# Seven passes for VectorE's exponentials, and six score banks a unit on VectorE in the final layer, in a four-layer attention kernel

## The chip, the core and the metric

The kernel runs on one core of a Trainium2 chip. The core has five engines with their own instruction queues: TensorE (PE, with its weight loads shown as PEld), VectorE (DVE), ScalarE (ACT), GpSimd (POOL) and SyncE (SP), and 16 DMA engines that they issue transfers to. TensorE writes its results into PSUM, eight banks of 128 partitions x 2 KB; a bank holds one 128x512 tile of fp32. The metric is device time in microseconds (us) of one launch, the median of several.

## The reference

The input is a sequence of 2048 rows of width 640, in bf16. Four layers run one after the other, A, B, A, B, each `x = x + attention(layernorm(x))`, with 32 heads of 20 elements. Layers A (numbers 0 and 2 in the kernel) let a query see only the 256 keys up to its own; layers B (1 and 3) let every query see all 2048 keys:

```python
scores = jnp.einsum("bhqd,bhkd->bhqk", q, k) * (Dh ** -0.5)
p = _softmax(scores, axis=-1)
o = jnp.einsum("bhqk,bhkd->bhqd", p, v)
return (lambda x, *d: x.transpose(*d))(o, 0, 2, 1, 3).reshape(B, S, D) @ wo
```

Each layer B takes 32 x 2048 x 2048 exponentials. They are the bulk of the elementwise work.

## The kernel before

**Units, banks and tiles.** Queries are cut into four chunks `c` of 512, heads into eight groups `g` of four. A *unit* is a layer, a chunk and a group, (l, c, g). In a layer B a unit has 16 key blocks x 4 heads = 64 *banks*: one bank is the scores of 128 keys against 512 queries of one head, transposed so that keys lie on partitions. A *tile* is usually three banks: TensorE writes the scores of three banks into PSUM (L1316; banks 0 to 2 on even tiles, 3 to 5 on odd ones), ScalarE takes the exponential of all three in one instruction and writes bf16 to SBUF (L1347), and two or three tiles later TensorE multiplies them by the values (L1380) and accumulates in bank 7. On odd tiles a fourth bank, number 6, can be added if nothing else wants it (`next_tile`); such a tile is an instruction of 2048 columns that writes `ka`.

**Bank 6** has three users in the final layer: those wide tiles, the short tasks that finish units (`t_tail`: row sums, reciprocals, scaling) and chunks (`t_out`, `t_before_last`: the output projection), which take it through `take_m` and give it back with `drop_m`, and the path described next.

**The side path.** Some banks of a unit, `u.aside`, never go to ScalarE. `t_side` is a generator that computes their exponentials on VectorE, two banks (a *pair*) at a time. For each of the two it has TensorE write the scores into bank 6 (L912, in layer 3) and reads them with L918, which scales to a fixed-point number, clamps and stores int32. Then six passes over the pair's 128x1024 elements follow, all SBUF to SBUF: L923 and L928 split mantissa and exponent with bit operations, L933, L937, L941 and L949 are two-input operations that evaluate a quartic; the last multiplies by the power of two and writes bf16. That is eight instructions to a pair. In layer 3 its scratch lies in idle `xnT` buffers, its results in five slots for pairs, three in `ka` and two in `qa`; in layer 1 it uses `raw_o`. The values of the aside banks are multiplied in at the end of the unit (L1389), and a unit's slots come free then.

**The order of the work.** The whole program is emitted by one Python loop, tile by tile (`state["tick"]`), and every engine runs its queue in that order. The side path is paced by a credit: after each tile it gains `SIDE_RATE` = 1.1 (0.95 in the last chunk of layer 3, 0.4 before the final stage), is capped at 1.2, and each pass costs what its `yield` says, 0.7 or 1.2. A score needs an odd tile, credit above zero and bank 6 free (`side_now`); after a score bank 6 counts as taken for two ticks. `side_need` and `side_done` push the side path on without credit if a unit ends before its aside banks are scored or finished. The side path may work on a unit as soon as that unit's keys are loaded, ahead of ScalarE, as long as it has slots.

Besides, TensorE gets filler matmuls (L298 with `masks,ident`, from `keep_clock`) so that each tile has a fixed amount of TensorE work. The units of layer 3 run last: (3,0,g) in two parts, then (3,1,0) to (3,3,7), 24 units, with nothing else beside them but their own finishing tasks.

**Which banks are aside.** In layer 1, chunks 1 to 3, two of a unit's 64. In layer 3, chunks 1 to 3, four of them in every unit but (3,1,0), which has none; and six in the units of chunks 1 and 2 with odd g, (3,2,7) excepted. That is 23 units x 4 + 7 x 2 = 106 banks, the count of L918 on `xnT` in the profile.

Of the kernel before, what the change touches and what calls it, by code (L numbers as in the profile page):

```python
# [9 lines left out]
BF16 = mybir.dt.bfloat16  # L10
F32 = mybir.dt.float32
I32 = mybir.dt.int32
ALU = mybir.AluOpType
ACT = mybir.ActivationFunctionType

# [5 lines left out]
NT = S // P  # L21
KD = D // P
G = 8
C = 512
NC = S // C
EPS = 1e-5
SCALE = DH ** -0.5
# [2 lines left out]

E23 = 2.0 ** 23
LOG2E = 1.4426950408889634
EA, EB, EC, ED = -0.10468731, 1.17604568, 0.83196789, 0.24582313
KA = 18
SIDE_RATE = 1.1
QA = 4

PARTS = {  # L40
# [6 lines left out]
def kernel(  # L47
# [58 lines left out]
    op = ps[:, 7, :]  # L106
# [565 lines left out]
    class Unit:  # L672
        def __init__(self, l, c, g, part=None):
            self.l, self.c, self.g, self.part = l, c, g, part
            self.windowed = l % 2 == 0
            self.aside = ()
            if self.windowed:
                sets = [(m, b0, subs, j) for m, b0, subs in window_banks(c) for j in range(4)]
            else:

                if c > 0 and (l, c, g) != (3, 1, 0):
                    self.aside = tuple((NT - 1, j) for j in ((2, 3) if l == 1 else range(4)))
                    if l == 3 and (c < 3 and g % 2 and (c, g) != (2, 7)):
                        self.aside += ((NT - 2, 0), (NT - 2, 1))
                    if l == 1 and False:
                        self.aside += ((NT - 1, 0), (NT - 1, 1))
                k0, k1 = key_blocks(l, part)
                sets = [
                    (None, 0, [(kc, 0, 4, 0)], j) for kc in range(k0, k1) for j in range(4)
                    if (kc, j) not in self.aside  # L690
                ]
            n = len(sets)
            self.banks = [
                (self, j, m, b0, subs, i < 4, i >= n - 4 + len(self.aside), i == n - 1)
                for i, (m, b0, subs, j) in enumerate(sets)
            ]
# [200 lines left out]
    def t_side():  # L897

        V = nc.vector
        while aside:  # L900
            u = aside[0]
            for pair in range(len(u.aside) // 2):
                while id(u) not in loaded or (u.l == 3 and not side["late"]):
                    yield None
                for i in range(2):
                    yield "bank"
                    xi, xm, xw = side["tiles"]
                    if u.l == 3:
                        mseq[0] += 1
                        mfree[6] = (state["tick"] + 2, mseq[0])  # L910
                        kc, j = u.aside[2 * pair + i]
                        nc.tensor.matmul(  # L912
                            ps[:, 6, :], lhsT=u.k(kc, j), rhs=u.q(j, 0, 4), start=True, stop=True
                        )
                        side["psum"] = ps[:, 6, :]
                    scored = side.setdefault("scored", {})
                    scored[id(u)] = scored.get(id(u), 0) + 1
                    V.tensor_scalar(  # L918
                        out=xi.bitcast(I32)[:, i * C : (i + 1) * C], in0=side["psum"],
                        scalar1=SCALE * LOG2E * E23, scalar2=-128.0 * E23, op0=ALU.mult, op1=ALU.max,  # L920
                    )
                    yield 0.7
                V.tensor_scalar(  # L923
                    out=xm.bitcast(I32), in0=xi.bitcast(I32), scalar1=0x7FFFFF, scalar2=0x3E800000,
                    op0=ALU.bitwise_and, op1=ALU.bitwise_or,
                )
                yield 0.7
                V.tensor_scalar(  # L928
                    out=xi.bitcast(I32), in0=xi.bitcast(I32), scalar1=0x7F800000,
                    scalar2=0x40000000, op0=ALU.bitwise_and, op1=ALU.bitwise_xor,  # L930
                )
                yield 0.7
                V.scalar_tensor_tensor(  # L933
                    out=xw, in0=xm, scalar=EA, in1=xm, op0=ALU.add, op1=ALU.mult
                )
                yield 1.2
                V.scalar_tensor_tensor(  # L937
                    out=xm, in0=xw, scalar=EB, in1=xm, op0=ALU.mult, op1=ALU.add
                )
                yield 1.2  # L940
                V.scalar_tensor_tensor(  # L941
                    out=xw, in0=xw, scalar=EC, in1=xm, op0=ALU.add, op1=ALU.mult
                )
                yield 1.2
                while not side["out"]:
                    yield None
                pt = side["out"].popleft()
                po = pt.rearrange("p a b -> p (a b)")
                V.scalar_tensor_tensor(  # L949
                    out=po, in0=xw, scalar=ED, in1=xi, op0=ALU.add, op1=ALU.mult  # L950
                )
                side_out.setdefault(id(u), []).append(pt)
                yield 1.2
            aside.popleft()

    def side_step(bank):

        if side["gen"] is None:
            return False
        moved = False  # L960
        while True:
            if side.get("at") == "bank" and not bank:
                return moved
            if side["credit"] <= 0.0:
                return moved
            try:
                at = side["at"] = next(side["gen"])
            except StopIteration:
                side["gen"] = None
                return moved  # L970
            if at is None:
                return moved
            moved = True
            if at == "bank":
                if not bank:
                    return moved
                continue
            side["credit"] -= at
            if bank:
                return moved  # L980

    def side_need(u):

# [219 lines left out]
    with tc.manual_schedule():  # L1203
# [40 lines left out]
        def next_tile(t):  # L1244

            if t < len(tiles):
                return tiles[t]
            size = 3
            if side_now:
                return [banks.popleft() for _ in range(min(size, len(banks)))]  # L1250
            if t % 2 and not tails and state["held"] is None and mfree[6][0] < state["tick"]:
                if all(task.wake > state["tick"] for task in todo):
                    size = 4
            return [banks.popleft() for _ in range(min(size, len(banks)))]

# [23 lines left out]
        while ended is None or t < ended + 8:  # L1279
# [119 lines left out]
                    break  # L1399

            if n_b:
                side["credit"] = min(side["credit"] + ((SIDE_RATE if state["unit"] < index[3, NC - 1, 0, None] else 0.95) if side["late"] else 0.4), 1.2)
                side_step(False)

            if t > 0 and masked is not None:
# [71 lines left out]
```

## Time and profile before

| | us |
|---|---|
| time, median of 3 runs | 2258.31 |
| the runs | 2255.68, 2258.31, 2261.54 |
| span of the profiled execution | 2253.6 |
| ACT busy in it | 2159.6 (96%) |
| PE busy | 1946.9 (86%) |
| DVE busy | 1253.3 (56%) |
| first score of the final layer's side path (L918 on `xnT`) | starts at 1599.0 |
| last ACT instruction | 2241.8 to 2242.5 |

The profile gives the span from the first to the last instruction; the median of the timed runs is 4.7 us above the span. PE's busy time holds the filler matmuls. In group lines a row is: line, engine, operation, output <- input, shapes, count | busy us in all, mean ns of one | idle us of the engine before them and who ended it. Instructions of one engine overlap a little, so busy time divided by count is less than the mean duration of one. In window lines a row is the stretch in us from the span's start, its length, and the busy us (and instructions) of each engine, then TensorE's granted clock and the DMA's share.

### The profile page before, as it was taken

The numbers are of one execution on the slowest core, as the hardware profiler recorded it, in microseconds if no ns is written. First come the engines' busy times: TensorE is split into PE (matmuls) and PEld (weight loads), VectorE is DVE, ScalarE is ACT, GpSimd is POOL, SyncE is SP. The second block draws the span as 40 slices with busy tenths as digits, with TensorE's granted clock in tenths as the row PEclk, the third lists the DMA queues.
The fourth block names the chain that finished last, engine by engine and source line by source line (L and its number), as shares of the span: only waits on it lengthen the run. The fifth ranks groups of instructions, "written<-read, shape, count | busy, mean of one in ns | idle before, by whom it ended". The sixth has DMA issues, their size and how long they took to land.

```text
span 2253.6 us, 71223 instructions
## 1 busy us (share of the span) xinstructions
PE 1946.9 (86%) x30991; PEld 775.9 (34%) x30991; DVE 1253.3 (56%) x2150; ACT 2159.6 (96%) x1736; POOL 484.2 (21%) x950
## 2 busy tenths in 40 slices
PE   8999998988888888888888888898888888888887
PEld 4444443334333333333333443342322222222222
DVE  6656564436454555455553643242577667776666
ACT  7899899999999999999899999999999999999997
POOL 6674544201111124111331123312000000000000
PEclk9999999999999999999999999999999999999999
DMA  6233323422111233012320143113211111111100
GB/s 196 74 102 84 91 78 91 104 70 69 54 34 28 65 91 87 15 34 62 97 78 15 23 115 95 29 26 89 64 52 31 31 40 34 31 31 47 39 19 16
DMA packets 88408, 137.15 MB, mean 61 GB/s; under 512 B 20766, under 2 KB 63486, under 8 KB 88094
## 3 DMA queue, kind: packets, MB, share of 16 engines
q1 hardware_dynamic: 68878, 79.43, 13.2%
q0 software_dynamic: 19216, 53.17, 8.1%
q8 instruction: 242, 3.96, 0.8%
q14 instruction: 72, 0.59, 0.1%
HBM read 99.52 MB, written 27.79 MB: 56 GB/s over the span
## 4 chain that ended last, share of the span: by engine, by line
ACT 46%; PE 25%; issue 16%; DVE 10%; POOL 1%; DMA 1%; SPq 0%; ACTq 0%; DVEq 0%; POOLq 0%
ACT pt L1347 44%; PE ps L298 15%; PE ps L1316 6%; PE ps L1380 2%; ACT ka L1347 1%; DVE on L1092 1%; DVE st L321 1%; DVE x_sb L566 1%; PE ps L1088 1%; PE ps L435 1%; DVE pt L1429 1%; DVE va L321 1%; DVE vs L321 0%; DVE xnT L937 0%; DVE xnT L933 0%
## 5 line engine op out<-in xcount | busy, mean ns | idle before, releaser
L1347 ACT ACTIVATE pt<-ps 128x1536 bf16<-128x1536 f32 (+2 forms) x1634 | 2085.3, 1456 | 62.2 <-PE ps L1316 50.8
L298 PE MATMUL ps<-masks,ident 128*32 128x512 bf16 x6420 | 551.6, 388 | 114.3 <-ACT pt L1347 59.9
L1316 PE MATMUL ps<-qt,kt 32*128 32x512 bf16 x3990 | 545.3, 384 | 92.7 <-ACT pt L1347 84.9
L1380 PE MATMUL ps<-pt,vt 128*21 128x512 bf16 x3838 | 393.2, 382 | 0.1
L1316 PEld LDWEIGHTS <-kt 32*128 32x128 bf16 x3990 | 165.0, 91 | 551.4 <-issue 536.1
L1419 POOL TENSOR_SCALAR_AFFINE_SELECT pt<-pt 128x256 bf16<-128x256 bf16 (+2 forms) x505 | 216.3, 450 | 373.6 <-ACT pt L1347 333.1
L298 PEld LDWEIGHTS <-ident 128*32 128x32 bf16 x6420 | 165.9, 94 | 363.0 <-issue 350.0
L298 PE MATMUL ps<-xnT,wqk 128*32 128x512 bf16 x3320 | 220.6, 383 | 16.3 <-DVE st L321 8.1
L1429 DVE TENSOR_TENSOR pt<-pt,masks 128x512 bf16<-128x512 bf16 (+4 forms) x267 | 114.3, 440 | 177.7 <-ACT pt L1347 175.9
L321 DVE CAST st<-ps 128x512 bf16<-128x512 f32 x134 | 92.7, 692 | 197.9 <-PE ps L298 197.7
L298 PE MATMUL ps<-wop,on 128*32 128x320 bf16 x3712 | 156.9, 301 | 13.9 <-DVE x_sb L566 8.8
L918 DVE TENSOR_SCALAR xnT<-ps 128x512 int32<-128x512 f32 x106 | 73.3, 692 | 163.2 <-PE ps L912 162.3
L1316 PE MATMUL ps<-qa,ka 32*128 32x384 bf16 (+2 forms) x1408 | 118.2, 277 | 32.6 <-ACT pt L1347 29.7
L1380 PEld LDWEIGHTS <-vt 128*21 128x21 bf16 x3942 | 105.7, 91 | 115.3 <-issue 74.4
L298 PEld LDWEIGHTS <-on 128*32 128x32 bf16 x5760 | 116.6, 95 | 76.2 <-issue 54.1
L1092 DVE TENSOR_TENSOR on<-on,ps 128x512 bf16<-128x512 bf16 x128 | 86.4, 684 | 72.9 <-PE ps L1088 71.0
L298 PE MATMUL ps<-wv,xnT 128*32 128x320 bf16 x2560 | 112.4, 301 | 9.7 <-DVE on L1092 2.2
L566 DVE TENSOR_TENSOR x_sb<-x_sb,ps 128x320 bf16<-128x320 bf16 x120 | 58.2, 485 | 107.6 <-PE ps L298 107.5
L298 PEld LDWEIGHTS <-wqk 128*32 128x32 bf16 x3320 | 79.6, 96 | 110.9 <-issue 59.3
L864 DVE CAST on<-ps 128x512 bf16<-128x512 f32 x112 | 77.0, 687 | 44.4 <-PE ps L1380 29.7
L1316 PEld LDWEIGHTS <-ka 32*128 32x128 bf16 x1408 | 43.6, 92 | 116.7 <-issue 108.9
L402 POOL TENSOR_SCALAR rstd<-mv 128x4 f32<-128x4 f32 x15 | 3.7, 249 | 363.8 <-DVE mv L389 355.6
(101 smaller groups left out, 1655.3 us busy)
## 6 DMA issues: line engine op xcount, KB each, us to landing
vt<-v_d SPq DMA_DIRECT2D x48, 336.0 KB
kt<-k_d SPq DMA_DIRECT2D x192, 80.0 KB
wqk<-in_B_wqkv_dram POOLq DMA_DIRECT2D x80, 160.0 KB, 3.5
wqk<-in_A_wqkv_dram POOLq DMA_DIRECT2D x70, 160.0 KB, 3.6
k_d<-st POOLq DMA_DIRECT2D x75, 128.0 KB, 2.5
q_d<-st POOLq DMA_DIRECT2D x75, 128.0 KB, 2.5
qt<-q_d SPq DMA_DIRECT2D x384, 20.0 KB
v_d<-vs POOLq DMA_DIRECT2D x16, 336.0 KB, 3.6
```

What stands on the lines that cost most here:

```text
L298: nc.tensor.matmul(out_[r], lhsT=lhsT[:, r], rhs=rhs, start=start, stop=stop)
L321: nc.vector.tensor_copy(out=out_, in_=in_)
L435: nc.tensor.transpose(out=trp[32 * j : 32 * j + 32, dc, :], in_=xn[:, a : a + 32], identity=ident[:],)
L566: nc.vector.tensor_tensor(out=xv, in0=had, in1=yp, op=ALU.add)
L864: nc.vector.tensor_copy(out=oT, in_=op)
L918: V.tensor_scalar(out=xi.bitcast(I32)[:, i * C : (i + 1) * C], in0=side["psum"], scalar1=SCALE * LOG2E * E23, scalar2=-128.0 * E23, op0=AL ...
L1092: nc.vector.tensor_tensor(out=oT, in0=oT, in1=zb, op=ALU.mult)
L1316: nc.tensor.matmul(sp[:, i, col * P : (col + qn) * P], lhsT=u.k(kc, j), rhs=u.q(j, q0, qn), start=True, stop=True,)
L1347: nc.scalar.activation(out=pt[:, i:k, b0 * P :], in_=sp[:, i:k, b0 * P :], func=ACT.Exp, scale=SCALE,)
L1380: nc.tensor.matmul(op[32 * j : 32 * j + VW, q0 * P : (q0 + qn) * P], lhsT=u.v(kc, j), rhs=pg[:, i, col * P : (col + qn) * P], start=(first ...
L1419: nc.gpsimd.affine_select(out=v, in_=v, compare_op=ALU.is_gt if later else ALU.is_ge, fill=0.0, base=0, pattern=[[0, k - i], [-1 if later ...
L1429: nc.vector.tensor_tensor(out=pt_[:, i:k, cols], in0=pt_[:, i:k, cols], in1=mv_, op=ALU.mult)
```

## The change

Three things change.

1. The exponential of a pair takes seven instructions. L918 scales by 2^16 in place of 2^23, so the int32 holds the integer part of the exponent in its upper halfword and the fraction in its lower one. One pass reads the lower halfwords (every second uint16) and writes a linear function of the fraction as fp32; one reads the upper halfwords (every second int16) and writes the bit pattern of the bf16 power of two, contiguous int16; two two-input passes evaluate a cubic, the second writing bf16 to the slot; one bf16 x bf16 multiplication applies the power, in place.
2. Six banks are aside in every unit of layer 3's chunks 1 to 3 but the first (none) and the last, (3,3,7) (four): 22 x 6 + 4 = 136 banks.
3. The credit per tile is 1.2 (was 1.1), 1.1 in the last chunk (was 0.95), the cap 1.3 (was 1.2). `next_tile` makes no wide tile where one of the next four banks is the last of a unit whose aside banks aren't all scored.

```diff
-E23 = 2.0 ** 23
+FIX = 2.0 ** 16
 LOG2E = 1.4426950408889634
-EA, EB, EC, ED = -0.10468731, 1.17604568, 0.83196789, 0.24582313
+E1, E0, EA, EB = 6.520200689873914e-06 * FIX, 0.7855486869812012, -1.118533968925476, 1.5344765186309814
 KA = 18
-SIDE_RATE = 1.1
+SIDE_RATE = 1.2
...
                 if c > 0 and (l, c, g) != (3, 1, 0):
                     self.aside = tuple((NT - 1, j) for j in ((2, 3) if l == 1 else range(4)))
-                    if l == 3 and (c < 3 and g % 2 and (c, g) != (2, 7)):
+                    if l == 3 and (c, g) != (NC - 1, G - 1):
                         self.aside += ((NT - 2, 0), (NT - 2, 1))
...
                     V.tensor_scalar(
                         out=xi.bitcast(I32)[:, i * C : (i + 1) * C], in0=side["psum"],
-                        scalar1=SCALE * LOG2E * E23, scalar2=-128.0 * E23, op0=ALU.mult, op1=ALU.max,
+                        scalar1=SCALE * LOG2E * FIX, scalar2=-127.0 * FIX, op0=ALU.mult, op1=ALU.max,
                     )
                     yield 0.7
                 V.tensor_scalar(
-                    out=xm.bitcast(I32), in0=xi.bitcast(I32), scalar1=0x7FFFFF, scalar2=0x3E800000,
-                    op0=ALU.bitwise_and, op1=ALU.bitwise_or,
+                    out=xm, in0=xi.bitcast(U16)[:, 0::2],
+                    scalar1=E1 / FIX, scalar2=E0, op0=ALU.mult, op1=ALU.add,
                 )
                 yield 0.7
+                power = xw.bitcast(I16)[:, 0 : 2 * C]
                 V.tensor_scalar(
-                    out=xi.bitcast(I32), in0=xi.bitcast(I32), scalar1=0x7F800000,
-                    scalar2=0x40000000, op0=ALU.bitwise_and, op1=ALU.bitwise_xor,
+                    out=power, in0=xi.bitcast(I16)[:, 1::2],
+                    scalar1=127.0, scalar2=128.0, op0=ALU.add, op1=ALU.mult,
                 )
                 yield 0.7
                 V.scalar_tensor_tensor(
-                    out=xw, in0=xm, scalar=EA, in1=xm, op0=ALU.add, op1=ALU.mult
-                )
-                yield 1.2
-                V.scalar_tensor_tensor(
-                    out=xm, in0=xw, scalar=EB, in1=xm, op0=ALU.mult, op1=ALU.add
-                )
-                yield 1.2
-                V.scalar_tensor_tensor(
-                    out=xw, in0=xw, scalar=EC, in1=xm, op0=ALU.add, op1=ALU.mult
+                    out=xi, in0=xm, scalar=EA, in1=xm, op0=ALU.add, op1=ALU.mult
                 )
                 yield 1.2
                 while not side["out"]:
...
                 V.scalar_tensor_tensor(
-                    out=po, in0=xw, scalar=ED, in1=xi, op0=ALU.add, op1=ALU.mult
+                    out=po, in0=xi, scalar=EB, in1=xm, op0=ALU.add, op1=ALU.mult
                 )
+                yield 1.2
+                V.tensor_tensor(out=po, in0=po, in1=power.bitcast(BF16), op=ALU.mult)
                 side_out.setdefault(id(u), []).append(pt)
-                yield 1.2
+                yield 0.7
...
+    def side_left(u):
+        return u in aside and side.get("scored", {}).get(id(u), 0) < len(u.aside)
...
             if t % 2 and not tails and state["held"] is None and mfree[6][0] < state["tick"]:
-                if all(task.wake > state["tick"] for task in todo):
+                if all(task.wake > state["tick"] for task in todo) and not any(
+                    b[-1] and side_left(b[0]) for b in list(banks)[:4]
+                ):
                     size = 4
...
-                side["credit"] = min(side["credit"] + ((SIDE_RATE if state["unit"] < index[3, NC - 1, 0, None] else 0.95) if side["late"] else 0.4), 1.2)
+                side["credit"] = min(side["credit"] + ((SIDE_RATE if state["unit"] < index[3, NC - 1, 0, None] else 1.1) if side["late"] else 0.4), 1.3)
```

More of the change, by code (lines that the diff above doesn't have):

```diff
@@ L12 @@
 I32 = mybir.dt.int32
+I16 = mybir.dt.int16
+U16 = mybir.dt.uint16
 ALU = mybir.AluOpType
@@ L682, in __init__ @@
                     self.aside = tuple((NT - 1, j) for j in ((2, 3) if l == 1 else range(4)))
-                    if l == 3 and (c < 3 and g % 2 and (c, g) != (2, 7)):
+                    if l == 3 and (c, g) != (NC - 1, G - 1):
                         self.aside += ((NT - 2, 0), (NT - 2, 1))
-                    if l == 1 and False:
-                        self.aside += ((NT - 1, 0), (NT - 1, 1))
                 k0, k1 = key_blocks(l, part)
```

## The prediction, made before the changed kernel was run

> **What bounds the kernel now.** I read the page first: the busy sums, then the 40 slices, to find the stage that the change is about.
>
> ```profile
> PE 1946.9 (86%) x30991; PEld 775.9 (34%) x30991; DVE 1253.3 (56%) x2150; ACT 2159.6 (96%) x1736; POOL 484.2 (21%) x950
> ...
> DVE  6656564436454555455553643242577667776666
> ACT  7899899999999999999899999999999999999997
> POOL 6674544201111124111331123312000000000000
> PEclk9999999999999999999999999999999999999999
> ```
>
> A slice is 56 us. From slice 29 on POOL does nothing: that is the final layer. ACT stands at 9 throughout and DVE at 6 to 7. Next, the busy time by stretches: chunks 1, 2 and 3 of the final layer, as near as ACT's start times give their borders, and one short stretch inside the first.
>
> ```profile
> 1624.00:1812.00 188.00, 160.97 (x2072) 50.02 (x2067) 136.12 (x163) 185.37 (x136) 0.00 (x0) 0.98 0.14 39
> 1812.00:2026.00 214.00, 181.11 (x2371) 56.01 (x2367) 158.11 (x193) 213.10 (x156) 0.00 (x0) 1.00 0.13 36
> 2026.00:2214.00 188.00, 158.42 (x2090) 51.74 (x2087) 119.20 (x152) 187.61 (x138) 0.00 (x0) 1.00 0.12 33
> ...
> 1765.00:1785.00 20.00, 17.98 (x188) 4.74 (x180) 14.29 (x19) 18.00 (x15) 0.00 (x0) 0.83 0.05 13
> ```
>
> The fourth busy column is ACT: 586.1 of 590 us, and half of the missing 3.9 lies in the 20 us where the granted clock fell to 0.83. DVE has 136 of 188, 158 of 214 and 119 of 188. The waits between the first ACT instruction of unit (3,1,0), 1594, and the last of all say the same:
>
> ```profile
> ACT pt L1347 <- PE ps L1316: 3.6, 9, 0.9
> ```
>
> So ACT's own work sets the pace of the final layer: a bank taken from it is worth its time, as long as the bank's new home keeps up. The groups by shape, from 1560 on, price both homes:
>
> ```profile
> L1347 ACT ACTIVATE pt<-ps 128x1536 bf16<-128x1536 f32 x468 | 638.1, 1549 | 4.6 <-PE ps L1316 3.6
> L1347 ACT ACTIVATE ka<-ps 128x2048 bf16<-128x2048 f32 x26 | 52.0, 1998 | 0.0
> L918 DVE TENSOR_SCALAR xnT<-ps 128x512 int32<-128x512 f32 x106 | 73.3, 692 | 163.2 <-PE ps L912 162.3
> L933 DVE SCALAR_TENSOR_TENSOR xnT<-xnT 128x1024 f32<-128x1024 f32 x53 | 64.6, 1218 | 0.0
> L923 DVE TENSOR_SCALAR xnT<-xnT 128x1024 int32<-128x1024 int32 x53 | 36.7, 693 | 1.6
> L1092 DVE TENSOR_TENSOR on<-on,ps 128x512 bf16<-128x512 bf16 x32 | 21.8, 683 | 13.3 <-PE ps L1088 13.3
> L864 DVE CAST on<-ps 128x512 bf16<-128x512 f32 x24 | 16.5, 686 | 4.8 <-PE ps L1389 4.6
> ```
>
> A score bank costs DVE 0.69 us, a two-input fp32 pass of a pair 1.22, a one-input pass 0.69; DVE's idle time in front of L918 (162 us) is room, not delay.
>
> **Fewer banks on ACT.** 136 banks aside in place of 106 are 30 fewer for ACT. First price: from ACT's start of (3,1,0), 1594.3, to the end of its last instruction, 2242.5, it does 24 x 64 - 106 = 1430 banks in 648.2 us, 0.453 each; 30 x 0.453 = 13.6 us. Second price: the trace holds units of both sizes. Counting ACT's starts off in banks, the seven units with six aside last 26.1 us on average (26.3, 26.7, 24.9, 26.5, 27.2, 25.0, 26.2), their neighbours with four, without the one that holds the clock's dip, 27.0 (27.0, 27.2, 26.1, 27.3, 27.9, 26.3), and the last chunk's 26.9. A pair moved is worth 0.8 to 0.9; 15 pairs are 11 to 13.6 us. I take 13.
>
> **The passes.** Before, a pair is 2 x 0.692 (L918) + 2 x 0.693 (L923, L928) + 4 x 1.22 = 7.65 us. After: 2 x 0.692, two one-input passes over halfwords, 2 x 1.22, and a bf16 product. The trace shows no one-input pass at a stride of two halfwords; it lies between L923's 0.69 (same elements, one input, SBUF to SBUF) and L933's 1.22 (same elements, two inputs). I take 0.69, since L923 has the same number of inputs and the same span read. The bf16 product at 1024 columns follows from the masks' products, which are of its kind:
>
> ```profile
> L1429 DVE TENSOR_TENSOR pt<-pt,masks 128x512 bf16<-128x512 bf16 x98 | 45.1, 462 | 57.2 <-ACT pt L1347 56.3 <-POOL pt L1419 0.7
> L1429 DVE TENSOR_TENSOR pt<-pt,masks 128x768 bf16<-128x768 bf16 x58 | 34.1, 588 | 62.9 <-ACT pt L1347 62.7
> L1429 DVE TENSOR_TENSOR pt<-pt,masks 128x256 bf16<-128x256 bf16 x91 | 30.0, 337 | 56.1 <-ACT pt L1347 55.8
> ```
>
> 0.125 us more per 256 columns: 0.71; at worst L933's 1.22. A pair is then 1.38 + 1.39 + 2.44 + 0.71 = 5.92 us, at worst 7.5.
>
> [...]
>
> **Does DVE keep up?** Three pairs a unit are 17.8 us (20.9 at 1.22 for both strided passes; 22.4 with the slow product too); the rest of DVE's work in a unit, L864, L1092, L566 and the small tail operations, some 65 us over 24 units, is 2.7. Together 20.5 (at worst 25.1) in a unit of 58 banks x 0.453 = 26.3. Before, a six-bank unit needed 23 + 2.7 and lived on the four-bank units beside it. 68 pairs x 5.92 = 403 us against 53 x 7.65 = 405: DVE is as busy as it was.
>
> **Does the order keep up?** A pair's credit is 4 x 0.7 + 2 x 1.2 + 0.7 = 5.9 (was 7.6). Walk it: the second score leaves 0.6; after that tile's credit (cap 1.3) the two halfword passes go out, leaving -0.1; the next tile takes one two-input pass, the next the other, the next the product, and the following odd tile has credit for a score. So 2 tiles between scores and 4 after: 6 a pair at 1.2, and also at 1.1 (0.1 is left at the end). The same walk for before gives 8 at 1.1 and 10 at 0.95, and the L918 starts show it: pairs begin mostly 10 to 11.5 us apart in chunks 1 and 2, 13.4 to 14.3 in chunk 3, at 1.36 us a tile. A unit of 58 banks has 19.3 tiles; three pairs need 18. Besides, the side path begins at 1599.0, 25 us before (3,1,1) reaches ACT, and may fill five slots ahead. So the passes are hidden beside ACT with 1.3 tiles to spare a unit and a lead of some two pairs. If that cover goes, the last pair of a unit is pushed out at its end, and ACT waits (first rival).
>
> **What else moves.** Inside the 6-tile cycle bank 6 counts as free for the other users in 2 ticks, and never on the odd tile that a wide tile needs; wide tiles fall from 26 to few. One instruction for four banks starts 1.757 us before the next, three take 1.331 (medians of ACT's starts): per bank 0.439 against 0.444, so losing all 26 costs 104 x 0.005 = 0.5 us; I put it inside the 13 taken. TensorE does the same products, 30 scores through L912 in place of L1316, and fillers by the tile, so its 85% stays; POOL is idle. The stores and packing transfers on SP's queue follow the finishing tasks, later if these wait for bank 6; two sets of `on` allow eight units' time, and the last chunk's partial projection (L597, last at 2225.9) had 16 us before ACT's end. The new condition on wide tiles acts only where the side path is late.
>
> **Layer 1** has 24 pairs with the new passes: 24 x 1.73 = 42 us less on DVE between 493 and 1302. ACT waits there 18 us for scores, TensorE in turn some 25 us for DVE's evacuations. DVE is busy some 420 us there, so a tenth of its load goes; a tenth of 18 is 1.8, nothing at the low end, since no score waits on these passes in the planner. I take 1.
>
> **Sum.** 13 + 1 = 14 us off the profiled execution's 2253.6 span, so 2239.6; the same off the median, which stands 4.7 above that span: 2244.3.
>
> **Rivals.**
> *Bank 6 runs short (slower).* Six scores, four tail steps per two units and eight projection steps per chunk share one bank. In favour: where the projection ran (L566, 1845 to 1863), pairs of (3,2,1) began 16.7 us apart in place of 11, and side pairs in chunk 3 ended 5 us, later 3 and at last none, before their unit's last ACT tile began. Against: one such delay per chunk, 5.5 us, is within the lead. It decides once a pair needs more than 19.3 / 3 = 6.4 tiles on average; then the lead is eaten and the last pair is forced: two scores and passes, about 2 x (0.37 + 0.69) + 4.5 = 6.6 us, less the 3 tiles (4.1) by which the value products lag, 2.5 us of ACT idle a unit. Ten units: +25 - 14 = 2269.
> *Half the gain.* The clock dips oftener (the dip at 1771 cost ACT 2.0 us) or units stall at their ends for 0.3 us each: 3 dips or 22 x 0.3 take 6 to 7 of 14: 2251.
> *The strided passes are slow.* At 1.22 DVE still fits (23.6 of 26.3) and only evacuations come 0.5 us later: 2246. Only at 2.2 us or more each does DVE exceed the unit (22.3 + 4 + 2.7 above 26.3), and nothing in the trace suggests it.
> *Layer 1 gains more.* If half of ACT's 18 us there were behind DVE's long passes: 2236.
>
> **How the numbers follow.** Forecast (2240 to 2249, slow strided passes included) 0.73; half the gain 0.11; bank 6 short 0.10; layer 1 gains more 0.06. Within 0.3% (6.8 us, about what this measurement can tell from nothing) counts as no change: the border is 2251.5. The forecast and layer 1 give faster 0.79 and half of "half the gain" 0.05; same gets the other 0.05 and a mild shortage of bank 6, 0.03; slower the rest, 0.08. The range, 2237 to 2254, takes in the price bounds (11 to 13.6, layer 1 from 0 to 9) and half the gain, and leaves out the shortage.
>
> **What would show it.** Right: L918 on `xnT` 136 times, pairs 8.2 us apart, halfword passes at 0.69 and the product at 0.71, ACT's busy time from 1594 down by 13 and its waits still under 6 us, DVE's idle before L918 still the largest wait. Wrong: ACT waiting for L1316 at the units' ends, TensorE waiting for the new product before L1389, pairs 9 us apart or more, halfword passes above 0.7, or a lower clock in the final layer.

## The result

The changed kernel takes 2251.29 us, median of 15 runs (2244.86 to 2258.51); the kernel before took 2256.50, median of 15 beside it. The ratio is 0.9973, 95% interval 0.9962 to 0.9983: 0.27% or 6 us faster, where 14 us were forecast. The time lies inside the stated range; the gain is less than half of the forecast, and below the 0.3% that was called clear of no change. The profiled execution took 2252.22 us (span 2250.5).

### The profile after

The page of the changed kernel: the busy sums, and the slices of DVE, ACT and the clock.

```profile
PE 1959.8 (87%) x30915; PEld 773.2 (34%) x30915; DVE 1201.6 (53%) x2178; ACT 2147.6 (95%) x1734; POOL 485.4 (22%) x950
...
DVE  6656564435343554345453533242567767767774
ACT  7899899999999999999899999999999999999997
...
PEclk9999999999999999999999999999999999999999
```

ACT lost 12 us of work, DVE 52; the slices look as before. The groups by shape from 1555 on show that the new passes cost what was forecast:

```profile
L918 DVE TENSOR_SCALAR xnT<-ps 128x512 int32<-128x512 f32 x136 | 93.6, 688 | 134.7 <-PE ps L912 123.6 <-PE ps L1316 10.8
L934 DVE SCALAR_TENSOR_TENSOR xnT<-xnT 128x1024 f32<-128x1024 f32 x68 | 83.3, 1225 | 2.3
...
L923 DVE TENSOR_SCALAR xnT<-xnT 128x1024 f32<-128x1024 uint16 x68 | 47.2, 694 | 2.2
L929 DVE TENSOR_SCALAR xnT<-xnT 128x1024 int16<-128x1024 int16 x68 | 46.7, 687 | 0.0
...
L946 DVE TENSOR_TENSOR ka<-ka,xnT 128x1024 bf16<-128x1024 bf16 x42 | 28.9, 688 | 1.0
```

136 scores, both halfword passes at 0.69, the product at 0.69; pairs begin 8.4 us apart (median of their first scores), where 8.2 were forecast. So the change did what it says, and DVE is not short: it idles 134.7 us in front of L918. The time is lost in the waits of the final layer, 1590 to 2240; ACT's, and the one of TensorE that has no counterpart in the kernel before:

```profile
ACT pt L1347 <- PE ps L1316: 12.1, 15, 3.5
...
PE ps L300 <- DMA on<-on: 6.3, 2, 3.5
```

ACT waits 12.1 us for scores in place of 3.6, and TensorE stops twice, 6.3 us in all, because the output projection (L300 with `wop,on`; the helper stood at L298 before) finds rows of `on` that have not arrived. These rows are written by the packing transfers of `settle` (L1103). TensorE's timeline at the first stop, and SP's queue just ahead of it (start, duration, line, what):

```profile
1846.41 0.39 PE L1316 MATMUL ps<-qt,kt 32*128 32x512 bf16 x3
1846.73 0.73 PE L300 MATMUL ps<-wop,on 128*32 128x320 bf16 x16
1850.95 0.32 PE L300 MATMUL ps<-wop,on 128*32 128x320 bf16 x4 [3.49 <-DMA on<-on]
```

```profile
1838.37 0.35 SPq L778 DMA_DIRECT2D vt<-v_d  x1
...
1842.37 0.33 SPq L792 DMA_DIRECT2D kt<-k_d  x1
1842.80 6.83 SPq L1103 DMA_DIRECT2D on<-on  x9
```

The nine packing transfers stand behind the nine loads of the next unit, and take SP 6.8 us to issue. In the kernel before, the same stretch of SP's queue has them the other way round:

```profile
1828.15 9.47 SPq L1105 DMA_DIRECT2D on<-on  x9
1841.95 0.36 SPq L778 DMA_DIRECT2D vt<-v_d  x1
```

After this stop the granted clock is lower, 0.80 in the 25 us around it. The window of the changed kernel (stretch, length, busy PE, PEld, DVE, ACT, POOL, granted clock, DMA):

```profile
1845.00:1870.00 25.00, 20.57 (x230) 5.91 (x230) 15.37 (x21) 19.21 (x15) 0.00 (x0) 0.80 0.07 20
```

ACT works 19.2 of these 25 us. The clock record has 10.2 us at half speed from 1851.6, and 3.4 us from 2066.6, behind the second stop; two more of 3.4 us, at 1814 and 2234, stand away from them.

The final layer's stretch on ACT, from its first instruction of (3,1,0) to the end of its last, went from 648.2 us to 644.3. Thirty banks at 1.331 / 3 us (the median between ACT's starts, as before) are 13.3 less; what the starts exceed this median by, summed, rose from 13.6 to 22.5 us, and 3.7 and 3.0 of that rise are the two stops. The stretch before the final layer ends at 1595.1 and ended at 1594.3. One profile can't tell more of it: in the seven runs below that have the changed kernel's code up to there it ends between 1590.7 and 1597.9.

### The profile page after: what moved, and what is told of

The parts are those of the page before. It is cut to its first block, busy times and chain, and to the rows that moved or that the text cites. A ratio compares the mean times of both kernels' runs of the same rounds, so it can differ in the third digit from the quotient of the medians.

```text
span 2250.5 us, 71088 instructions
## 1 busy us (share of the span) xinstructions
PE 1959.8 (87%) x30915; PEld 773.2 (34%) x30915; DVE 1201.6 (53%) x2178; ACT 2147.6 (95%) x1734; POOL 485.4 (22%) x950
## 4 chain that ended last, share of the span: by engine, by line
ACT 47%; PE 26%; issue 16%; DVE 9%; POOL 1%; DMA 1%; SPq 1%; ACTq 0%; DVEq 0%; POOLq 0%
ACT pt L1347 46%; PE ps L300 16%; PE ps L1316 6%; PE ps L1380 2%; DVE st L323 1%; DVE x_sb L568 1%; DVE on L1090 1%; DVE va L323 1%; DVE pt L1429 1%; PE ps L1086 1%; DVE vs L323 0%; DVE raw_o L934 0%; PE ps L437 0%; DVE xnT L323 0%; SPq L1103 0%
## 5 line engine op out<-in xcount | busy, mean ns | idle before, releaser
L1347 ACT ACTIVATE pt<-ps 128x1536 bf16<-128x1536 f32 (+2 forms) x1656 | 2110.4, 1448 | 70.4 <-PE ps L1316 58.0
L300 PE MATMUL ps<-masks,ident 128*32 128x512 bf16 x6344 | 549.7, 390 | 101.3 <-ACT pt L1347 58.2
L1380 PE MATMUL ps<-pt,vt 128*21 128x512 bf16 x3904 | 397.9, 383 | 0.3 <-ACT pt L1347 0.2
L300 PEld LDWEIGHTS <-ident 128*32 128x32 bf16 x6344 | 165.5, 94 | 342.6 <-issue 332.0
L300 PE MATMUL ps<-xnT,wqk 128*32 128x512 bf16 x3320 | 221.6, 384 | 16.4 <-DVE st L323 7.9
L300 PE MATMUL ps<-wop,on 128*32 128x320 bf16 x3712 | 157.7, 302 | 17.1 <-DMA on<-on 6.3
L918 DVE TENSOR_SCALAR xnT<-ps 128x512 int32<-128x512 f32 x136 | 93.6, 688 | 134.7 <-PE ps L912 123.6
L300 PEld LDWEIGHTS <-on 128*32 128x32 bf16 x5760 | 116.8, 95 | 80.6 <-issue 58.3
L1090 DVE TENSOR_TENSOR on<-on,ps 128x512 bf16<-128x512 bf16 x128 | 86.4, 684 | 68.6 <-PE ps L1086 66.6
L300 PE MATMUL ps<-wv,xnT 128*32 128x320 bf16 x2560 | 112.5, 301 | 10.2 <-DVE on L1090 2.2
L300 PEld LDWEIGHTS <-wqk 128*32 128x32 bf16 x3320 | 79.9, 96 | 111.6 <-issue 58.8
L864 DVE CAST on<-ps 128x512 bf16<-128x512 f32 x112 | 77.0, 688 | 69.9 <-PE ps L1389 38.1
L934 DVE SCALAR_TENSOR_TENSOR xnT<-xnT 128x1024 f32<-128x1024 f32 x68 | 83.3, 1225 | 2.3
```

Of the source, the lines that this page charges most:

```text
L300: nc.tensor.matmul(out_[r], lhsT=lhsT[:, r], rhs=rhs, start=start, stop=stop)
L864: nc.vector.tensor_copy(out=oT, in_=op)
L918: V.tensor_scalar(out=xi.bitcast(I32)[:, i * C : (i + 1) * C], in0=side["psum"], scalar1=SCALE * LOG2E * FIX, scalar2=-127.0 * FIX, op0=AL ...
L934: V.scalar_tensor_tensor(out=xi, in0=xm, scalar=EA, in1=xm, op0=ALU.add, op1=ALU.mult)
L1090: nc.vector.tensor_tensor(out=oT, in0=oT, in1=zb, op=ALU.mult)
L1347: nc.scalar.activation(out=pt[:, i:k, b0 * P :], in_=sp[:, i:k, b0 * P :], func=ACT.Exp, scale=SCALE,)
```

## The experiments

Two theories were put against each other first. *Q*: the order on SP's queue causes the stops, and the stops the dips of the clock. *F*: the new mix of work on TensorE, with two wide tiles left of 26, lets the clock dip oftener by itself.

### The packing transfers on another queue

```diff
-                    nc.sync.dma_start(
+                    nc.gpsimd.dma_start(
                         out=on[o : o + n, b, :], in_=oT[32 * j + a : 32 * j + a + n, :]
```

> The changed kernel, with the packing transfers of a finished unit (on<-on, in settle) issued on POOL's queue, which is idle in the final layer, in place of SP's. Theory Q (queue order): in the changed kernel these transfers stand behind the next unit's nine loads on SP's queue, so that the chunk's projection finds them not landed, TensorE stops for 3.5 and 2.9 us, ACT starves for 3.7 and 3.0 us, and the clock dips that follow (10.2 and 3.4 us at half) cost some more. Then TensorE's wait for DMA on<-on goes below 1 us in all, ACT's stretch in the final layer falls from 644 to 637 or less, and the ratio to the kernel before goes from 0.997 to 0.993 to 0.9945. Theory F (fillers): the lost time comes from the new mix of work on TensorE (two wide tiles left of 26, more scores through bank 6), which lets the clock dip oftener wherever it may. Then the DMA wait may go, but the dips stay at 17 us or more at half clock in the final layer and the ratio stays at 0.996 to 0.9975. Above 0.998 if issuing on POOL costs what it saves.

Measured: 0.9941 (0.9921 to 0.9961). The wait for `on<-on` is gone, ACT's stretch is 633.0 us, no clock dip lies between 220 and 2233 us of the profiled execution (mean clock 0.999). The edit touches neither tiles nor fillers nor wide tiles (two, as before it); F has no room for this.

### The projection later

```diff
             if g == G - 1 or (l, c, g) == (3, NC - 1, G - 3):
-                yield ("wait", 3)
+                yield ("wait", 9)
```

> The changed kernel, with the projection of a chunk pushed nine ticks after its last packing transfers are issued in place of three (8 us later); SP's queue keeps its order. Theory Q: the transfers land 3.5 and 2.9 us after TensorE wants them, six ticks of 1.36 us cover that, so the wait for DMA on<-on goes to nothing and the ratio to before falls to 0.993 to 0.9945, as with the other queue. Theory F: 0.996 to 0.9975, dips unchanged. If the projection, now later, runs into the next unit's end instead, ACT shows a new wait of 1 us or more there.

Measured: 0.9928 (0.9909 to 0.9947), 2240.71 us. The waits of ACT in the final layer and its groups there:

```profile
ACT pt L1347 <- PE ps L1316: 2.0, 5, 0.9
```

```profile
L1347 ACT ACTIVATE pt<-ps 128x1536 bf16<-128x1536 f32 x466 | 629.1, 1534 | 2.9 <-PE ps L1316 2.0 <-ACT pt L1347 0.2
```

The stretch is 632.8 us, 15.4 less than before. SP's order is as in the changed kernel, only TensorE comes after the data. So it is the stop that costs, and this version beats both kernels.

### The projection sooner

```diff
-                yield ("wait", 3)
+                yield ("wait", 1)
```

> The changed kernel, with the projection pushed one tick after its last packing transfers are issued in place of three (2.7 us sooner); nothing else. If TensorE's stop for the packing transfers is what the changed kernel loses (theory Q), the two stops of 3.5 and 2.9 us grow by up to 2.7 us each, ACT's gaps with them, and the clock dips after them stay or grow: 5 us and some more, ratio 0.999 to 1.002 over the changed kernel's 0.997. If the stop is a symptom that something else covers, the ratio stays at 0.996 to 0.998.

Measured: 1.0030 (1.0020 to 1.0041), above the range given. The waits of TensorE for the transfers and of ACT in the final layer (the weight loads, PEld, wait in the same stops, so the rows don't add up):

```profile
PE ps L300 <- DMA on<-on: 17.6, 4, 4.9
...
PEld L300 <- DMA on<-on: 8.4, 2, 4.2
...
PE ps L591 <- DMA on<-on: 2.9, 1, 2.9
```

```profile
ACT pt L1347 <- PE ps L1316: 24.9, 10, 8.9
```

The two gaps of ACT grew from 3.7 and 3.0 to 8.7 and 9.1 us, more than the 2.7 each that the two ticks are worth, and a third of 3.1 appeared where the last chunk's partial projection (L591) now waits too. TensorE stops twice at each of the first two, for 3.9 and 4.9 us; why by so much more than two ticks was not taken apart. Clock dips stand at all three: 10.2 us from 1840.6, 13.7 from 2055.7, 3.4 from 2219.5; a fourth, 6.8 us from 2240.0, stands at none. In the two runs above, without these stops, no dip lies in the final layer's stretch (mean clock of the profiled executions 0.999 and 0.997, here 0.990).

### The control: the kernel before with the projection later

```diff
-                yield ("wait", 3)
+                yield ("wait", 9)
```

> The kernel before with the projection nine ticks after the packing transfers in place of three: the control for the edit that brought the changed kernel to 0.993. Before shows no wait of TensorE for these transfers, so theory Q expects no difference, 0.9985 to 1.001, a final layer of 648 us on ACT. If the later projection is worth something by itself (fewer conflicts at bank 6, say), 0.997 or less, and the gain of 0.993 is not the change's.

Measured: 1.0027 (1.0017 to 1.0038): slower, neither of the two expectations. Without a stop to remove, the edit only costs: the last chunk's partial projection is late (its last L597 starts at 2246.8, was 2225.9), and 15.3 us follow ACT's last instruction in place of 11.1; ACT's stretch is 651.7, with one gap of 2.5 us. So the 0.45% that the edit brings the changed kernel is not the edit's own worth.

### Why the order on SP's queue turned

Theory *B*: the side path books bank 6 in 4 ticks of its 6-tile cycle, and the finishing tasks, which need it four times to two units, come late. The ends of units (L864) and the scaling (L1090, L1092 before) speak for it. In the kernel before, unit (3,1,7) ends at 1815.9, its group's scaling runs at 1827.4 and 1833.9, the next unit ends, and its successor's loads go out, at 1842. DVE's rows of before:

```profile
1827.45 0.68 DVE L1092 TENSOR_TENSOR on<-on,ps 128x512 bf16<-128x512 bf16 x1
...
1833.94 0.68 DVE L1092 TENSOR_TENSOR on<-on,ps 128x512 bf16<-128x512 bf16 x1
...
1842.05 0.68 DVE L864 CAST on<-ps 128x512 bf16<-128x512 f32 x1
```

After, the unit ends at 1809.9, the scaling runs at 1829.7 and 1836.8, 20 and 27 us later in place of 11.5 and 18, and the next unit ends at 1838.4. DVE's timeline of the changed kernel shows scaling and unit end side by side, 1.6 us apart:

```profile
1829.72 0.67 DVE L1090 TENSOR_TENSOR on<-on,ps 128x512 bf16<-128x512 bf16 x1
...
1836.75 0.68 DVE L1090 TENSOR_TENSOR on<-on,ps 128x512 bf16<-128x512 bf16 x1
1838.38 0.69 DVE L864 CAST on<-ps 128x512 bf16<-128x512 f32 x1 [0.94 <-PE ps L1389]
```

The packing comes two ticks behind the scaling, hence behind the loads.

```diff
                         mseq[0] += 1
-                        mfree[6] = (state["tick"] + 2, mseq[0])
+                        mfree[6] = (state["tick"] + 1, mseq[0])
                         kc, j = u.aside[2 * pair + i]
```

> The changed kernel with bank 6 counted as taken for one tick after a score in place of two; the projection at three ticks as it was. It tells why the packing transfers came behind the loads: theory B says that the side path, now at a pair every 6 tiles, leaves bank 6 to the finishing tasks for 2 ticks in 6, so that the scaling (L1090) of a chunk's last units comes 20 and 27 us after the unit's end in place of 11.5 and 18, after the next unit's loads are issued. With one tick booked, the tasks get the even ticks between scores, the scaling comes at 12 to 19 us, the transfers are issued ahead of the loads, TensorE's wait for DMA on<-on is gone and the ratio falls to 0.993 to 0.995. If the order flips for another reason (units are shorter by 0.9 us, say), scaling stays late and the ratio at 0.996 to 0.998. TensorE will wait for DVE's read of bank 6 a little oftener; if that costs more than 0.5 us at each of some 45 tasks, the ratio rises above 0.998.

Measured: 0.9925 (0.9910 to 0.9940), 2241.55 us. Unit (3,1,7) ends at 1815.7, its scaling runs at 1825.3 and 1827.1, 10 and 11 us later, and SP's queue has the old order again, the loads waiting until 1842.79:

```profile
1826.05 6.83 SPq L1103 DMA_DIRECT2D on<-on  x9
...
1842.79 0.34 SPq L778 DMA_DIRECT2D vt<-v_d  x1
```

TensorE's wait for `on<-on` is 0.2 us, ACT's for scores 4.0. Theory B holds: one tick less on one bank, and the whole chain of late scaling, late packing, stops and the dips at them is gone; one dip of 3.4 us is left in the final layer, at 1646. The edit also brings wide tiles back, 47 in place of 2, but they are not what helps: the stretch is 635.0 us with them and 632.8 without in the version with the later projection. Two runs below agree with B. With the old credit the side path is slower in the last chunk, pairs 10.9 us apart: there the scaling follows the end of (3,2,7) by 11.7 and 13.2 us, and the packing goes out 13 us ahead of the loads. With the old banks and the new passes, pairs of a unit some 8 us apart, it follows the end of (3,1,7) by 17 and 24 us, behind the loads. So the order goes with the pace of the pairs; six banks in every unit aren't needed for it.

### The new passes and the new credit, with the old banks

```diff
-                    if l == 3 and (c, g) != (NC - 1, G - 1):
+                    if l == 3 and (c < 3 and g % 2 and (c, g) != (2, 7)):
```

The edit is this condition alone. The expectation names the old credit and cap, but the kernel that ran has the new ones (1.2, 1.1 in the last chunk, cap 1.3). So it shows the passes together with the credit; the passes alone were not run.

> The seven passes alone: banks aside, credit rates and cap as before (the new condition on wide tiles stays in, it acts only when the side path is late). ACT has as many banks as before. Prediction's step: DVE loses 1.73 us a pair, 42 us in layer 1 and some 90 us in the final layer, ACT gains about 1 us in layer 1 and nothing in the final one: ratio 0.999 to 1.000, ACT's stretch in the final layer 648. Rival: a lighter DVE frees the TensorE waits for evacuations in layer 1 and the final layer, 0.996 or less. If the changed order of the finishing tasks (theory Q) came from the passes and not from the six banks, this one shows TensorE waiting for DMA on<-on too, and a ratio above 1.

Measured: 1.0063 (1.0046 to 1.0080). A miss: with the banks as before, the lighter passes at the new credit make the kernel 14 us slower. The waits in the final layer name a load that was never waited for before:

```profile
PEld L912 <- DMA kt<-k_d: 10.9, 6, 3.9
PE ps L912 <- DMA kt<-k_d: 9.2, 6, 3.6
...
PE ps L300 <- DMA on<-on: 3.2, 1, 3.2
```

The first two rows are the same stops, seen on the weight load and on the matmul: some 11 us in all, not the 20 that the next expectation adds up. The third row answers the last sentence of the expectation above: once, the packing stands behind the loads here too. With four or six banks a unit and a shorter pair the side path is done early and takes up the next unit as soon as its loads are issued. Its score (L912) then stands in TensorE's queue ahead of the work that could go on, waiting for keys:

```profile
2006.58 0.39 PE L1316 MATMUL ps<-qt,kt 32*128 32x512 bf16 x3 [0.36 <-ACT pt L1347]
2010.63 0.60 PE L912 MATMUL ps<-qt,kt 32*128 32x512 bf16 x1 [3.65 <-DMA kt<-k_d]
```

That wait does not occur in the changed kernel. The starts of the pairs say why: here the side path pauses between most units from (3,1,4) on, the next pair beginning 17 to 21 us after the last, as one that has run out of loaded units; with six banks a unit no two pairs begin more than 14.1 us apart.

### The same, with keys landed

```diff
-                while id(u) not in loaded or (u.l == 3 and not side["late"]):
+                while id(u) not in loaded or (
+                    u.l == 3 and (not side["late"] or state["tick"] < loaded_at[id(u)] + 8)
+                ):
...
-                yield ("wait", 3)
+                yield ("wait", 9)
```

on top of the edit above, so again with the new credit; `loaded_at` holds the tick in which a unit's loads are issued.

> The seven passes alone, once more (banks aside and credit as before), but in the final layer the side path may begin a unit only eight ticks (11 us) after its loads are issued, and the projection comes nine ticks after the packing transfers. In the run of the passes alone the lighter side path caught up with the loads and TensorE stopped 20 us in all at its scores (L912) for the key transfers kt<-k_d. If that and the packing wait were all of its loss of 0.6%, then both waits are gone, ACT's stretch in the final layer is 647 to 649 us, and the ratio is 0.998 to 1.0005: the passes by themselves are worth nothing to ACT. If DVE's relief matters, 0.997 or less; if the passes cost something of their own, above 1.002.

Measured: 0.9987 (0.9977 to 0.9996). Both waits are gone, ACT waits 1.3 us for scores, the stretch is 644.7 us, a little under the expected 647 to 649. So the two waits, with what follows them, were the loss. By the interval, the passes with the new credit are worth 1 to 5 us while ACT has its old banks; what of that is the passes', the credit's or the later projection's (which costs the kernel before 0.27%) was not separated. The rest of what the version with the later projection gains (0.72% in all) comes with the six banks.

### Six banks with the old passes

The kernel before, with

```diff
-                    if l == 3 and (c < 3 and g % 2 and (c, g) != (2, 7)):
+                    if l == 3 and (c, g) != (NC - 1, G - 1):
...
-SIDE_RATE = 1.1
+SIDE_RATE = 1.6
...
-else 0.95) if side["late"] else 0.4), 1.2)
+else 1.6) if side["late"] else 0.4), 1.7)
...
-                yield ("wait", 3)
+                yield ("wait", 9)
```

and the new condition on wide tiles.

> Six banks a unit with the eight old passes, a credit of 1.6 (cap 1.7) that would allow a pair every 6 tiles, and the projection nine ticks after the packing transfers. DVE would need 3 x 7.65 + 2.7 = 25.7 us in a unit of 26.3, so the prediction's sum of DVE's load says it is at its limit: TensorE waits for L918 to free bank 6 and for the last pass before the aside values, ACT's waits grow to 10 to 40 us, ratio 0.997 to 1.01. If it comes out at 0.993 like the changed kernel with the later projection, the new passes weren't needed for the six banks and only the pace was.

Measured: 1.0267 (1.0253 to 1.0281), worse than expected. ACT's waits in the final layer, and some of TensorE's:

```profile
ACT pt L1352 <- PE ps L1321: 58.7, 79, 2.1
```

```profile
PE ps L298 <- DVE rT L1074: 13.3, 10, 1.7
PE ps L298 <- DVE rz L1056: 12.1, 9, 1.6
...
PE ps L912 <- DVE xnT L918: 8.4, 17, 1.0
```

No single long stop: TensorE waits short times all over (1.7 us at most in these rows), for small operations of DVE, in whose queue the passes of 1.22 us stand. Half-clock time in the stretch is 99 us. So the old passes don't carry six banks, as the sum of the prediction (25.7 us of DVE work in 26.3) had it. But DVE isn't full: it is busy 546 of 670 us between 1620 and 2290. How much of the loss is DVE's queue, and how much the clock, was not separated.

### The old credit

```diff
-SIDE_RATE = 1.2
+SIDE_RATE = 1.1
...
-((SIDE_RATE if state["unit"] < index[3, NC - 1, 0, None] else 1.1) if side["late"] else 0.4), 1.3)
+((SIDE_RATE if state["unit"] < index[3, NC - 1, 0, None] else 0.95) if side["late"] else 0.4), 1.2)
```

> The changed kernel with the old credit: 1.1 a tile, 0.95 in the last chunk, cap 1.2. By the walk in the prediction a pair then takes 8 tiles (10 in the last chunk) where a unit of 58 banks has 19.3 for three: the lead of 25 us is used up after some five units, then the last pair of a unit is pushed out at its end. The prediction's first rival prices that at 2.5 us of ACT idle a unit: 17 units, 42 us, ratio 1.012 to 1.02 over the changed kernel's 0.997. If forced passes are hidden behind the lag of the value products, the ratio stays at 0.997 to 1.000.

Measured: 0.9998 (0.9985 to 1.0010), 0.25% above the changed kernel, inside the expectation's second range. The shortage is there, in TensorE's wait for the last product of a pair before the aside values:

```profile
PE ps L1389 <- DVE ka L946: 6.3, 3, 2.2
PE ps L300 <- DMA on<-on: 2.9, 1, 2.9
...
PE ps L1389 <- DVE qa L946: 1.7, 1, 1.7
```

8.0 us in four waits. But the expectation used the wrong pace: 8 and 10 tiles a pair are the prediction's walk for the old passes; for the new ones it gives 6, "and also at 1.1". So it came out: up to 2020 pairs begin 9.0 us apart on average, as in the changed kernel, and only in the last chunk, at 0.95, 10.9 (8 tiles) in place of 8.9. All four waits stand there, at the ends of (3,3,3) to (3,3,6), one unit after the other, and ACT's starts come 2.1, 1.8, 2.3 and 2.6 us late at them. That is near the 2.5 us a unit that the first rival took for a shortage; it was the 17 units of the expectation that were too many. Of ACT's 20.9 us of waits in all, 3.0 are a stop for `on<-on` at the first chunk's projection.

### Four banks aside in layer 1 as well

On the version with the later projection:

```diff
-                    self.aside = tuple((NT - 1, j) for j in ((2, 3) if l == 1 else range(4)))
+                    self.aside = tuple((NT - 1, j) for j in range(4))
...
-                and len(tiles) >= 3 * len(at) + (at or [0])[0]
+                and len(tiles) >= 5 * len(at) + (at or [0])[0]
...
-if side["late"] else 0.4), 1.3)
+if side["late"] else 0.9), 1.3)
```

> The changed kernel with the projection nine ticks after the packing transfers, and besides four banks a unit aside in layer 1's chunks 1 to 3 (was two), a side bank put into a tile every five tiles (was three), credit 0.9 a tile there (was 0.4). 24 x 2 = 48 more banks leave ACT. In layer 1 a side bank takes the place of a bank in a tile, so the number of ACT's instructions stays and only 512 columns of each go: between the starts of one wide instruction and one of three banks lie 1.757 - 1.331 = 0.43 us a bank, 20 us at most if ACT sets the pace there as in the final layer. DVE gets 24 x 5.9 = 142 us more in some 800, where it is busy half the time and evacuates for TensorE. If ACT's work is the bound in layer 1 too: ratio 0.984 to 0.988. If TensorE, DVE's evacuations or the tasks' order are (ACT waits 18 us there as it is): 0.989 to 0.994, with ACT's waits for scores growing in layer 1.

Measured: 0.9979 (0.9969 to 0.9988), above both ranges: the extra banks lose what the later projection won. Between 490 and 1300 ACT is busy 767.6 us in place of 789.7, but it waits 40.2 us for scores in place of 15.4:

```profile
ACT pt L1347 <- PE ps L1316: 40.2, 83, 1.6
```

In layer 1 ACT alone doesn't set the pace; whether TensorE's own work, DVE's evacuations or the clock (27 us at half between 490 and 1300, 3.4 in the version with the later projection) stand in the way was not separated. The price "a bank off ACT is 0.45 us" was shown for the final layer alone.

## Why the prediction was right or wrong

- **What bounds the final layer: right.** Without the stops the stretch is 15.4 us shorter (632.8 against 648.2) for the 13 that were taken. The first price, 13.6, was the nearer one; 13.3 of it is bank time, the rest lies in waits of ACT (2.0 for 3.6 us), of which before has 1.9 us at its one clock dip there.
- **The price of the passes: right.** 0.694, 0.687 and 0.69 us where 0.69, 0.69 and 0.71 were taken. The halfwords at a stride of two ran at the pace of the whole words, 0.694 and 0.687 us beside 0.693 (L923 before), as the prediction took it from that row.
- **Whether DVE and the order of the side path keep up: right.** Pairs fit, and no score and no product is waited for at a unit's end. The old credit brings the shortage in the last chunk, where a pair takes 8 tiles, more than the 6.4 that the prediction set as the border, and at near the price that it took; the old passes fail by more than the sum says. One sum is off without consequence: with strided passes of x us a unit needs 3 x (4.53 + 2x) + 2.7 us of DVE, which passes 26.3 at 1.67 us, not at 2.2.
- **"What else moves": the step that failed.** It says of the packing transfers on SP's queue that they follow the finishing tasks, "later if these wait for bank 6; two sets of `on` allow eight units' time", and costs that at nothing. The eight units are the time until `on` is needed again; the projection of the same rows is pushed three ticks after the packing is issued, whatever stands in front of it on SP. The prediction had the premise, bank 6 free in 2 ticks of 6, and drew the wide tiles from it, not the delay of the finishing tasks. The runs put in its place: scaling 8 to 9 us later, packing behind nine loads, two stops with 6.7 us of ACT's time, and the clock dips behind them.
- **The size of the loss.** The version without the stop is 0.45% faster than the changed kernel by the two ratios, some 10 us. 6.7 of it is seen in the trace. The rest fits the clock: in the 15 runs of the changed kernel the span grows by 0.32 us for each us at half clock (worked out from each run's span and mean clock; correlation 0.81), and their mean clock is 0.9915, 38 us at half clock, where six runs of the later projection have 0.9953, 21 us (and three sets of runs of the kernel before 0.9934 to 0.9943); 17 us more, so 5 to 6 us by the fit, a little over the 10 with the 6.7. That dips come with these stops is shown by the runs that remove them (no dip in the final layer's stretch in two of three, one of 3.4 us in the third) and lengthen them (10.2 and 13.7 us at half clock, 10.2 and 3.4 in the changed kernel); the 0.32 is a fit.
- **The rivals.** "Half the gain", at 0.11, gave 2251 and named more dips of the clock or stalls at unit ends: its time came out, its stalls were at the projection. "Bank 6 runs short" looked at the right bank from the wrong side: the side path took the bank, and the finishing tasks starved.
- **Layer 1: the 1 us taken is not resolved.** Between 490 and 1300 DVE has 41 us less (384.3 for 425.1, with the later projection), and ACT waits 15.4 us for scores in place of 17.6. But the same code ends the stretch before the final layer anywhere between 1590.7 and 1597.9, so one profile of each can't show 1 us.

## What to carry to other kernels

When one user of a shared bank or queue speeds up, walk the other users' steps too, up to the last instruction that waits for them: here the delay went from a bank to a small scaling, to a transfer, past a queue of loads, to a matmul that had been pushed at a fixed distance. A fixed distance between issuing a transfer and using it is only as good as the place of that transfer in its queue (here three ticks behind nine loads, and TensorE stopped for 3.5 and 2.9 us); where a prediction says "later", it has to say who reads the result and when. And a freed engine is not harmless: with the old banks, the lighter passes at the new credit made the kernel slower (1.0063) because the side path ran up against loads that had only just been issued.

## What the runs showed of the hardware

- A stop of TensorE of 3.5 us was followed by 10.2 us at half clock and one of 2.9 us by 3.4 us (changed kernel), one of 2.9 us by 10.2 us (old credit), and two pairs of stops of 3.9 and 4.9 us came with 10.2 and 13.7 us (sooner projection). The next longest stop of TensorE in the changed kernel's final layer, 1.6 us at 2087, has no dip at it. Dips stand without such a stop too: 6.8 us at 1771 in the kernel before, 3.4 us at 1814 in the changed one. Of the three versions of the changed kernel without the stop two have no dip in the final layer's stretch and the third one of 3.4 us. By the 0.32 us above, an estimate, the two stops of the changed kernel cost their own length and two thirds of it again (0.32 x 13.6 us on 6.3).
- Nine packing transfers between tiles in SBUF occupied SP for 6.83 us (changed kernel, from 1842.80), 0.76 from one to the next on average, where the starts of the loads beside them from DRAM lie 0.37 to 0.40 us apart, but for one of 1.34.
